# Attention and a routed expert layer on one core: the instruction order planned anew, the last pair's moves by engine copies, and another dependency for the first GpSimd rotation

## The chip, the core and the metric

The kernel runs on one core of a Trainium2 chip. A core has a matrix engine (PE), and VectorE (DVE), ScalarE (ACT) and GpSimd (POOL) for work on tiles; SyncE (SP) here issues DMA transfers. Each engine takes its own instructions strictly in order and waits at an instruction until the data that it needs are there. The metric is the device time of one execution in microseconds (us). Before the change its median was 584.03 us over 3 runs (583.14 to 585.76).

## The reference

For 8 batches, 8 heads, 576 positions and 64 values per head: q and k are turned by position, attention is computed per head, and the heads of a position are put side by side to rows of 512. Then, in each batch, the 128 rows with the highest gate score go through a two-layer network and are added, weighted, to themselves.

```python
def _attn_ref(q, k, v):
    ...
    q_rot, k_rot = (rotate(q), rotate(k))
    scores = (1.0 / np.sqrt(D)) * np.matmul(q_rot, k_rot.transpose(0, 1, 3, 2))
    scores = scores - np.max(scores, axis=-1, keepdims=True)
    attn = np.exp(scores)
    attn = attn / (np.sum(attn, axis=-1, keepdims=True) + 1e-09)
    return np.matmul(attn, v)
def _moe_ref(x, w_gate, w1, w2, capacity):
    scores = np.einsum('bsd,d->bs', x, w_gate)
    out = x.copy()
    for b in range(B):
        top_idx = np.argpartition(-scores[b], capacity)[:capacity]
        xe = x[b, top_idx]
        ye = np.maximum(xe @ w1, 0.0) @ w2
        g = 1.0 / (1.0 + np.exp(-scores[b, top_idx]))
        out[b, top_idx] = x[b, top_idx] + g[:, None] * ye
```

## The kernel before

The work is cut into 32 pairs of heads, four pairs to a batch.

**Rotation.** For each pair k and q come by DMA (L481) into one buffer each, `k_in` and `q_in`. POOL multiplies them by the tables (L504), adds the halves (L510, L514), ACT rounds the sum to a high part (L519), and POOL subtracts that to make a low part (L520, tiles `kl` and `ql`). For pair 0 DVE does this in smaller pieces.

**Scores.** A score step (L570) multiplies high and low parts, three products, for two of the nine row groups of a pair, or for the one that both heads share; a pair has five steps. DVE takes the row minimum of the negated scores (L591), ACT the exponential (L599), and DVE turns the result into `pt` in blocks of 32 (L622).

**Moves.** In each of a pair's two areas of `pt` two blocks must change their partitions. ACT or POOL copies one aside (L628), and four DMA moves per area on SP's queue do the change (L654). For the second area of the last pair the moves are copies of 32 partitions by ACT or POOL instead (L639), two for each half of each row group.

**Values and rows.** One value product for each area (L681), copied out (L356, L358), turned back to rows (L734), divided by the sums (L749, L753) and stored. The value tile `vt` also needs a copy to other partitions (L476), by ACT or POOL.

**Experts.** After each fourth pair come the gate scores (L821), a transpose for routing (L831), counting (L840, L853), a selection (L888) and the index products (L896). POOL casts the index (L911) and gathers the rows (L912) by an indirect DMA into `xe`; PE transposes them (L930), three-term expert products follow (L958, L977), DVE adds the result (L993), and POOL scatters the rows (L997). `xe` is a single buffer, so a gather cannot start until the scatter before it has read it. The experts' products of one batch are spread over the score steps of the next pairs. The weights get high and low parts during the first pairs (ACT L1022, POOL L1024).

**The order.** The code records every operation with a cost on each engine that may do it, a key (a due time, from `KEY`) and the operations that it comes after. `Order.run` then plays these costs forward, gives each free engine the ready operation with the lowest key, and so fixes both the order on each queue and which engine does a piece. The keys of each pair get random noise of 300 from a list of seeds, `SEEDS`. Where PE would be idle and has been busy for less than a share `warm` of a window, the plan puts in dummy matmuls (L367). `LANDED` is the time that the plan adds to the end of a transfer. The dependencies given to the plan decide the order alone: what an instruction waits for on the chip is set afterwards, from the tiles that it reads and writes.

The list that this change touches first is filled in `rotate` of pair 0, and read for pair 1:

```python
            if first:
                last_first.append(y)
...
        wait = list(last_first) if pi == 1 else []
```

Here `y` is a sum (L510, L514) and `d` the low part (L520).

Of the kernel before, what the change touches and what calls it, by code (L numbers as in the profile page):

```python
# [20 lines left out]
EPS = 1e-9  # L21


KEY = dict(warm=0.86, warm0=20000, warm1=1000000, dummy=430, dcols=256, ahead=15000, lag=16000, rem=400, value=17500, rows=5250, load=30500, rotate=173549, half=2500,
           gate=10237, route=21900, count=23781, select=5425, turn=24609, step=11400, count_=24062, select_=3000, turn_=98437, step_=10820, last_step=4750, kstep=2700, hold=3,
           vcopy=6000, lift=range(9), lifted=688, patience=900, over=450, near=-900, swap=9750, vsplit=9, vstep=2250, recip=7500, pool_lo=1, esplit=1, t_most=4, ring="SP", vring="SP", wring="SP", issue=250, svc0=800, svc1=200, svck=2101, svcq=2251, svcv=1501, first_moves=True, over_dma=750, patience_dma=1150)


SEEDS = (65, 53, 848, 188, 64, 106, 182, 56, 412, 765, 334, 840, 49, 811, 920, 630, 707, 350, 158, 580, 649, 829, 598,
         159, 606, 89, 919, 466, 149, 808, 916, 981, 466)  # L30
NOISE = 300.0


# [11 lines left out]
class Order:  # L45
# [4 lines left out]
    SEM = 45.0  # L50
    BLOCK, FETCH = 256, 3900.0
    WINDOW, FALL, RISE = 3413.0, 0.58, 0.88
    LANDED, FLYING = 500.0, 8


    TURN = {(a, b): t for t, froms, tos in (
# [222 lines left out]
def attention_moe_kernel(ctx: ExitStack, tc: tile.TileContext, q, k, v, gate, w1, w2, rope, outs, shape, cap):  # L279
# [32 lines left out]
    n_pairs = B * NP  # L312
# [146 lines left out]
    last_first = []  # L459
# [29 lines left out]
    def rotate(pi):  # L489
# [12 lines left out]
        def part(use, sum_use, sum_, tab, hu, lu, c0, c1, got, more=0):  # L502
            x, n = use.tile, c1 - c0
            m = op(time(2 * n), lambda: e.tensor_tensor(  # L504
                x[:, :, c0:c1], x[:, :, c0:c1], tab[:, :, c0:c1], op=ALU.mult), key + more, got)
            edge = name == "q" and c1 == S

            def add():
                m1 = MAIN if edge else c1
                e.tensor_tensor(sum_[:, c0:m1], x[:, 0, c0:m1], x[:, 1, c0:m1], op=ALU.add)  # L510
                for h in range(2) if edge else ():
                    hp = slice(64 * h, 64 * h + 64)
                    a, b = (x[hp, i, MAIN:S].rearrange("p (a j) -> p a j", j=32) for i in range(2))
                    e.tensor_tensor(striped(sum_)[hp, :, h], a, b, op=ALU.add)  # L514

            y = op(time(n) if not edge else {"DVE": dve(n, 1, 200.0)} if first else {"POOL": pool(MAIN, 540.0)}, add, key + more, [m] + sum_use.before)
            d1 = KW if edge else c1
            n = d1 - c0
            c = op({"ACT": act(n)}, lambda: nc.scalar.copy(hu.tile[:, c0:d1], sum_[:, c0:d1]), base + more, [y] + hu.before)  # L519
            d = op(time(n), lambda: e.tensor_tensor(  # L520
                lu.tile[:, c0:d1], sum_[:, c0:d1], hu.tile[:, c0:d1].bitcast(F32), op=ALU.subtract), base + more + 3000 * first, [c] + lu.before)
            use.by(m, y), sum_use.by(y, c, d), hu.by(c, d), lu.by(d)
            if first:
                last_first.append(y)
            return c0, d1, [c, d]

        whole = ((0, S),)
# [18 lines left out]
    def attend(pi):  # L546
# [64 lines left out]
        def turn(u, key):  # L611

            c = 1 if u == 8 else u // 4
# [15 lines left out]

            y = op({"ACT": act(L, 30), "POOL": pool_copy(L)}, aside_of, key, [o] + side_[c].before)  # L630
            area[c].by(o, y), side_[c].by(y)
            if not c or pi < n_pairs - 1:
                return [o, y]
            for g in (0, 2):
                e, o_ = slice(32 * g, 32 * g + 32), slice(32 * g + 32, 32 * g + 64)
# [8 lines left out]
        def move(c, key, turns):  # L644
# [13 lines left out]

            up = {g: (slice(32 * g, 32 * g + 32), slice(32 * g + 32, 32 * g + 64)) for g in (0, 2)}
            turns = sum(turns, [])  # L660
            if c and pi == n_pairs - 1:
                return
            gone = {g: part(g, two[e, 1], two[o_, 0], turns) for g, (e, o_) in up.items()}
            for g, (e, o_) in up.items():
# [109 lines left out]
        step = PAIR / len(UNITS)  # L774
# [377 lines left out]
```

## Time and profile before

| | |
|---|---|
| timed runs, median of 3 | 584.03 us |
| profiled execution | 578.55 us |
| its span, first to last instruction | 576.5 us |
| granted PE clock, mean of the span | 0.99 |
| matmul instructions of L367 (dummies) | 95, as 190 records |
| moves of the last pair by DMA | 4 of 8 |

The profile is one execution. A row of the time line gives the start, the duration, the engine, the line, the operation with what it writes and reads, and in brackets the idle time of the engine just before it with what ended it. A matmul in float32 appears as two records. Rows that follow each other on one line are merged with a count.

### The profile page before, as it was taken

Reading aid. Unit: us, or ns where it says so; the run is one execution under the profiler, and the core shown is the slowest. Engines: PE = TensorE matmul, PEld = TensorE weight load, DVE = VectorE, ACT = ScalarE, POOL = GpSimd, SP = SyncE. Lnnn points to the kernel's source line nnn. Section 1 sums busy time; section 2 is a strip of 40 time slices with the busy share of each in tenths; the row PEclk is TensorE's granted clock in tenths of the full one; section 3 lists DMA queues with packets and bytes.
Section 4 is the critical chain, followed back from the end, with each engine's and each line's share of the span. In section 5 each row is a group of like instructions: output and inputs, shape, how many; then the busy total and the mean of one; then the engine's idle time right before and its main releaser. Section 6 shows DMA issues by size and latency. Waiting matters only on the chain.

```text
span 576.5 us, 19632 instructions
## 1 busy us (share of the span) xinstructions
PE 534.2 (93%) x7558; PEld 443.7 (77%) x7558; DVE 494.2 (86%) x1249; ACT 478.2 (83%) x1307; POOL 452.1 (78%) x489
## 2 busy tenths in 40 slices
PE   2799999999999899989999999986999899999996
PEld 1587787788788688878788877765888787888885
DVE  7887899999999899988999979994999898989331
ACT  4788899999997999889998979785898998979521
POOL 2989999999998987969897998857899688825310
PEclk9989999999999999999999999997999999999999
DMA  7477887888676866676777687764776768555210
GB/s 238 136 215 223 238 240 214 244 221 240 197 225 189 227 175 194 198 234 192 198 224 197 185 213 177 191 195 131 219 198 193 227 178 214 156 131 157 63 38 18
DMA packets 56957, 108.67 MB, mean 189 GB/s; under 512 B 7072, under 2 KB 37664, under 8 KB 56864
## 3 DMA queue, kind: packets, MB, share of 16 engines
q1 hardware_dynamic: 54768, 102.58, 63.4%
q0 software_dynamic: 1280, 4.20, 2.4%
q8 instruction: 59, 0.97, 0.7%
q10 hardware_dynamic: 816, 0.66, 0.4%
q14 instruction: 34, 0.28, 0.2%
HBM read 54.14 MB, written 11.53 MB: 114 GB/s over the span
## 4 chain that ended last, share of the span: by engine, by line
PE 31%; ACT 19%; DMA 14%; POOL 14%; issue 11%; DVE 9%; SPq 1%; POOLq 0%; DVEq 0%; ACTq 0%
PE ps L681 9%; PE ps L570 9%; ACT pab L599 8%; PE ps L958 7%; DMA out_dram<-xe,idx 5%; DVE pab L591 3%; POOL q_in L504 3%; DVE pt L622 3%; DMA pt<-pt 3%; DMA k_in<-k_dram 3%; ACT pt L628 3%; DMA xe<-out_dram,idx 3%; PE ps L734 2%; POOL k_in L504 2%; ACT vt L476 2%
## 5 line engine op out<-in xcount | busy, mean ns | idle before, releaser
L599 ACT ACTIVATE pab<-pab,nm 128x576 f32<-128x576 f32 x256 | 197.1, 773 | 19.8 <-DVE pab L591 18.4
L622 DVE STREAM_TRANSPOSE pt<-pab 128x576 f32<-128x576 f32 x256 | 189.5, 761 | 17.4 <-ACT pab L599 15.9
L591 DVE TENSOR_SCALAR_CACHE_REDUCE pab<-ps 128x576 f32<-128x576 f32 x256 | 181.0, 745 | 22.8 <-PE ps L570 22.5
L681 PE MATMUL ps<-pt,vt 64*64 64x128 f32 (+1 forms) x4608 | 158.7, 286 | 2.5 <-ACT gp L751 1.8
L681 PEld LDWEIGHTS ps<-pt,vt 64*64 64x64 f32 x4608 | 140.8, 133 | 17.0 <-issue 6.5
L570 PE MATMUL ps<-kh,qh 64*128 64x288 f32 (+1 forms) x576 | 89.3, 352 | 13.7 <-ACT qh L519 10.2
L628 ACT COPY pt<-pt 128x288 f32<-128x288 f32 x220 | 87.9, 431 | 13.8 <-DVE pt L622 8.6
L504 POOL TENSOR_TENSOR k_in<-k_in,tabs 128x1152 f32<-128x1152 f32 x31 | 82.7, 2666 | 16.5 <-DMA k_in<-k_dram 15.9
L570 PEld LDWEIGHTS ps<-kh,qh 64*128 64x128 f32 (+1 forms) x576 | 51.2, 190 | 47.5 <-issue 12.8
L504 POOL TENSOR_TENSOR q_in<-q_in,tabs 128x1152 f32<-128x1152 f32 x31 | 82.8, 2669 | 3.4 <-DMA q_in<-q_dram 3.0
L570 PE MATMUL ps<-kh,ql 64*128 64x288 f32 (+1 forms) x576 | 71.3, 299 | 3.9 <-POOL ql L520 2.0
L570 PE MATMUL ps<-kl,qh 64*128 64x288 f32 (+1 forms) x576 | 70.7, 296 | 0.0
L570 PEld LDWEIGHTS ps<-kh,ql 64*128 64x128 f32 (+1 forms) x576 | 53.8, 190 | 4.7 <-POOL ql L520 2.5
L958 PE MATMUL ps<-w,xt 128*128 128x512 f32 x192 | 54.4, 413 | 0.0
L570 PEld LDWEIGHTS ps<-kl,qh 64*128 64x128 f32 (+1 forms) x576 | 53.9, 191 | 0.0
L734 PE MATMUL ps<-turner,ot 128*128 128x136 f32 x320 | 50.0, 287 | 3.6 <-ACT ot L356 3.0
L958 PE MATMUL ps<-w,ht 128*128 128x512 f32 x192 | 52.3, 409 | 0.0
L367 PE MATMUL ps<-tabs,turner 128*128 128x256 f32 x190 | 51.9, 398 | 0.0
L734 PEld LDWEIGHTS ps<-turner,ot 128*128 128x128 f32 x320 | 43.1, 189 | 10.5 <-ACT ot L356 4.8
L520 POOL TENSOR_TENSOR ql<-q_sum,qh 128x640 fp32r<-128x640 f32 x31 | 48.4, 1560 | 2.0 <-ACT qh L519 2.0
L599 ACT ACTIVATION_READ_ACCUMULATOR pab<-pab,nm 128x1 f32 x256 | 49.0, 191 | 0.0
L520 POOL TENSOR_TENSOR kl<-k_sum,kh 128x576 fp32r<-128x576 f32 x31 | 44.1, 1423 | 3.2 <-ACT kh L519 2.5
(110 smaller groups left out, 775.7 us busy)
## 6 DMA issues: line engine op xcount, KB each, us to landing
pt<-pt SPq DMA_DIRECT2D x124, 180.0 KB
pt<-pt SPq DMA_DIRECT2D x128, 144.0 KB
k_in<-k_dram SPq DMA_DIRECT2D x31, 576.0 KB
q_in<-q_dram SPq DMA_DIRECT2D x31, 576.0 KB
vt<-v_dram SPq DMA_DIRECT2D x32, 288.0 KB
out_dram<-x SPq DMA_DIRECT2D x16, 512.0 KB
xe<-w_dram SPq DMA_DIRECT2D x8, 256.0 KB
h<-w_dram SPq DMA_DIRECT2D x8, 256.0 KB
```

The costliest lines, as they stand in the source:

```text
L367: nc.tensor.matmul(bank_of(b)[:, 0:KEY["dcols"]], ident, tabs[:, 0, 0:KEY["dcols"]], start=True, stop=True)
L476: (nc.gpsimd.tensor_copy if e == "POOL" else nc.scalar.copy)(use.tile[mine, 1], use.tile[there, 0])
L504: m = op(time(2 * n), lambda: e.tensor_tensor(x[:, :, c0:c1], x[:, :, c0:c1], tab[:, :, c0:c1], op=ALU.mult), key + more, got)
L520: d = op(time(n), lambda: e.tensor_tensor(lu.tile[:, c0:d1], sum_[:, c0:d1], hu.tile[:, c0:d1].bitcast(F32), op=ALU.subtract), base + more ...
L570: nc.tensor.matmul(bank_of(bs[i])[:, n, 0:HALF], lt, rt, start=start, stop=stop)
L591: nc.vector.tensor_scalar(halves, bank_of(b)[:, :, 0:HALF], -1.0, None, op0=ALU.mult, op1=ALU.min, accum_out=nm.tile[:, u:u + 1])
L599: lambda: nc.scalar.activation(halves, halves if lift else bank_of(b)[:, :, 0:HALF], AF.Exp, bias=nm.tile[:, u:u + 1], scale=-1.0 if lift ...
L622: nc.vector.transpose(into, src.rearrange("p (m w j) -> p m w j", w=2, j=32))
L628: (nc.gpsimd.tensor_copy if e == "POOL" else nc.scalar.copy)(apart(c)[:, to * L:to * L + L], two)
L681: nc.tensor.matmul(bank_of(acc)[64 * h:64 * h + 64, g, c0:c0 + 32 * n], vt.tile[gp_, h ^ g, (m - 1) % 2 * NT + (m - 1) // 2 if m else 2 * ...
L734: nc.tensor.matmul(bank_of(b)[:, W * i:W * i + W], ot.tile[:, i * P:i * P + P], turner, start=True, stop=True)
L958: nc.tensor.matmul(bank_of(bank), lhs.tile[:, a, c * P:c * P + P], w[w_][:, c, fs], start=(c == 0 and i == 0), stop=(c == n - 1 and i == 2))
```

## The change

Three edits of the code. Pair 0's low parts `d` join the sums in the list that pair 1's rotation comes after. The first area of the last pair is moved by copies (L639) too, so its four moves at L654 are gone and sixteen copies are new. And the plan's numbers are others: `LANDED`, 20 entries of `KEY` (a few of them: `warm`, `load`, `rotate`, `turn_`, the service times of transfers) and all seeds.

```diff
-KEY = dict(warm=0.86, warm0=20000, ..., rows=5250, load=30500, rotate=173549, half=2500,
+KEY = dict(warm=0.82, warm0=20000, ..., rows=3750, load=27500, rotate=216936, half=6250,
...
-    LANDED, FLYING = 500.0, 8
+    LANDED, FLYING = 1250.0, 8
...
             if first:
-                last_first.append(y)
+                last_first.extend((y, d))
             return c0, d1, [c, d]
...
             area[c].by(o, y), side_[c].by(y)
-            if not c or pi < n_pairs - 1:
+            if pi < n_pairs - 1:
                 return [o, y]
             for g in (0, 2):
...
             turns = sum(turns, [])
-            if c and pi == n_pairs - 1:
+            if pi == n_pairs - 1:
                 return
             gone = {g: part(g, two[e, 1], two[o_, 0], turns) for g, (e, o_) in up.items()}
```

In the built programs the dummies go from 95 to 80, the copies of 32 partitions from 14 to 24 on POOL and from 6 to 12 on ACT, the moves from 252 to 248. All other work is the same in kind and number, but for small pieces that go to another engine.

On DVE, in pair 0, where `ql_85` is the second low part of q and L591 the row minima (- before, + now):

```order
 L514 TENSOR_TENSOR q_sum_78<-q_in_75 64x2x32 x2
-L591 TENSOR_SCALAR pab_89,nm_101<-ps 128x576 x2
+L591 TENSOR_SCALAR pab_89,nm_101<-ps 128x576
 L520 TENSOR_TENSOR ql_85<-q_sum_78,qh_83 128x512
-L622 STREAM_TRANSPOSE pt_92<-pab_89 128x9x2x32 x2
-L591 TENSOR_SCALAR pab_90,nm_101<-ps 128x576 x2
```

The low part now stands between the first two row minima in place of behind them.

On POOL, at the fourth scatter (L997) and the fifth gather (L912), with the semaphores that each instruction waits for; DMASW7 is the scatter's. Before:

```order
L997 DMA out_dram<-xe_110,idx_114 576x512 [waits DVE_49,Pool_49]
L476 COPY vt_87<-vt_87 64x576 [waits DMAHW0_49,PE_49]
L628 COPY pt_92<-pt_92 128x288 [waits DMAHW4_49,DMAHW5_49,DVE_49,Pool_49]
L628 COPY pt_92<-pt_92 128x288 [waits DVE_49]
L716 COPY sums_99<-sums_99 32x1 [waits Activation_49]
L716 COPY sums_99<-sums_99 32x1 [waits DMASW7_49,Pool_49]
L716 COPY sums_99<-sums_99 32x1 x2
L911 CAST idx_113<-gg_117 128x1 [waits Pool_49]
L912 DMA xe_110<-out_dram,idx_113 128x512 [waits DMAHW3_49,DMAHW2_49,Pool_49]
L504 TENSOR_TENSOR q_in_75<-q_in_75,tabs 128x1152 [waits DMAHW3_49]
```

And at the same place now:

```order
L997 DMA out_dram<-xe_110,idx_114 576x512 [waits DVE_49]
L476 COPY vt_87<-vt_87 64x576 [waits DMASW7_49,DMAHW7_49,PE_49,Pool_49]
L628 COPY pt_92<-pt_92 128x288 [waits DVE_49,Pool_49]
L504 TENSOR_TENSOR q_in_75<-q_in_75,tabs 128x1152 [waits DMAHW1_49]
L911 CAST idx_113<-gg_117 128x1 [waits DVE_49]
L912 DMA xe_110<-out_dram,idx_113 128x512 [waits DMAHW0_49,Pool_49]
```

The wait for the scatter moved from a small copy to the first copy behind the scatter, and a q multiply came ahead of the gather.

On PE, ahead of the transposes of the fifth gather (L930). The value products (L681) of two areas, score steps (three rows of L570 each), rows out (L734) and dummies (L367). Before:

```order
L681 MATMUL ps<-pt_92,vt_88 64x128 x36
L570 MATMUL ps<-kh_79,qh_83 128x288 x4
L570 MATMUL ps<-kl_81,qh_83 128x288 x4
L570 MATMUL ps<-kh_79,ql_85 128x288 x4
L367 MATMUL ps<-tabs,turner 128x256
L734 MATMUL ps<-turner,ot_94 128x136 x2
L367 MATMUL ps<-tabs,turner 128x256
L570 MATMUL ps<-kh_80,qh_84 128x288 x4
L570 MATMUL ps<-kl_82,qh_84 128x288 x4
L570 MATMUL ps<-kh_80,ql_86 128x288 x4
L681 MATMUL ps<-pt_93,vt_88 64x160 x36
L930 MATMUL ps<-turner,xe_110 128x128 x4
```

And now:

```order
L681 MATMUL ps<-pt_92,vt_88 64x128 x36
L367 MATMUL ps<-tabs,turner 128x256
L570 MATMUL ps<-kh_80,qh_84 128x288 x4
L570 MATMUL ps<-kl_82,qh_84 128x288 x4
L570 MATMUL ps<-kh_80,ql_86 128x288 x4
L734 MATMUL ps<-turner,ot_94 128x136 x2
L681 MATMUL ps<-pt_93,vt_88 64x160 x36
L570 MATMUL ps<-kh_80,qh_84 128x288 x4
L570 MATMUL ps<-kl_82,qh_84 128x288 x4
L570 MATMUL ps<-kh_80,ql_86 128x288 x4
L930 MATMUL ps<-turner,xe_110 128x128 x4
```

A dummy went, and the second area's product now stands ahead of a score step that is the next pair's second in place of its first.

## Rows read from the trace of the kernel before

**Rows 1.** The page's busy times: engine, us, share of the span, instructions.

```profile
PE 534.2 (93%) x7558; PEld 443.7 (77%) x7558; DVE 494.2 (86%) x1249; ACT 478.2 (83%) x1307; POOL 452.1 (78%) x489
```

**Rows 2.** Groups by form, dummies: records, busy us, mean ns, idle before.

```profile
L367 PE MATMUL ps<-tabs,turner 128*128 128x256 f32 x190 | 51.9, 398 | 0.0
```

**Rows 3.** Time line of PE and POOL at pair 2 and pair 8.

```profile
46.30 0.53 PE L570 MATMUL ps<-kh,ql 64*128 64x288 f32 x4 [0.43 <-POOL ql L520]
...
133.92 1.57 POOL L520 TENSOR_TENSOR ql<-q_sum,qh 128x640 fp32r<-128x640 f32 x1
...
141.30 0.53 PE L570 MATMUL ps<-kh,qh 64*128 64x288 f32 x4
```

**Rows 4.** Busy us by engine, between index products: first, fourth, fifth cycle, sum.

```profile
119.60:182.50 62.90, 62.15 (x936) 52.25 (x935) 60.00 (x153) 57.92 (x159) 59.91 (x62) 1.00 0.77 224
...
311.40:376.80 65.40, 62.89 (x931) 52.07 (x929) 59.34 (x151) 55.94 (x158) 56.52 (x61) 1.00 0.74 199
376.80:447.40 70.60, 63.38 (x932) 53.14 (x931) 60.00 (x153) 57.51 (x156) 56.12 (x64) 0.95 0.66 186
...
sum 392.60, PE 374.50 PEld 312.56 DVE 358.94 ACT 346.39 POOL 330.17; mean PE 62.42 PEld 52.09 DVE 59.82 ACT 57.73 POOL 55.03
```

**Rows 5.** Waits of PE: us in total, times, longest.

```profile
PE ps L930 <- DMA xe<-out_dram,idx: 13.1, 4, 7.2
```

**Rows 6.** Time line of PE and POOL, fourth scatter to fifth gather.

```profile
367.51 2.34 PE L958 MATMUL ps<-w,ht 128*128 128x512 f32 x9
...
377.45 1.06 POOL L997 DMA_INDIRECT out_dram<-xe,idx  x1 [0.28 <-POOL q_sum L514]
...
385.76 0.61 POOL L716 COPY sums<-sums 32x1 f32<-32x1 f32 x3 [5.39 <-DMA out_dram<-xe,idx]
...
387.28 1.06 POOL L912 DMA_INDIRECT xe<-out_dram,idx  x1 [0.66 <-POOL idx L911]
...
393.55 1.11 PE L930 MATMUL ps<-turner,xe 128*128 128x128 f32 x4 [7.22 <-DMA xe<-out_dram,idx]
```

**Rows 7.** Time line of POOL and DVE in pair 0; group of the smaller low part.

```profile
12.78 2.64 POOL L504 TENSOR_TENSOR k_in<-k_in,tabs 128x1152 f32<-128x1152 f32 x1 [10.35 <-DMA k_in<-k_dram]
...
13.61 2.35 DVE L520 TENSOR_TENSOR ql<-q_sum,qh 128x512 fp32r<-128x512 f32 x1
...
L520 DVE TENSOR_TENSOR kl<-k_sum,kh 128x288 fp32r<-128x288 f32 x2 | 0.9, 454 | 0.5 <-ACT kh L519 0.5
```

**Rows 8.** Groups of POOL by form.

```profile
L504 POOL TENSOR_TENSOR q_in<-q_in,tabs 128x1152 f32<-128x1152 f32 x31 | 82.8, 2669 | 3.4 <-DMA q_in<-q_dram 3.0
...
L510 POOL TENSOR_TENSOR k_sum<-k_in 128x576 f32<-128x576 f32 x31 | 44.1, 1423 | 0.9
...
L628 POOL COPY pt<-pt 128x288 f32<-128x288 f32 x68 | 28.1, 427 | 15.7 <-DVE pt L622 9.1 <-issue 5.4
...
L1024 POOL TENSOR_TENSOR w<-h,w 128x512 fp32r<-128x512 f32 x8 | 10.3, 1287 | 0.9 <-ACT w L1022 0.9
```

**Rows 9.** Chain of waits: value products of the two areas, a score step.

```profile
370.32 2.61 PE ps L681 x72
372.92 0.99 PE ps L570 x12
...
402.18 2.12 PE ps L681 x72
```

**Rows 10.** Line L997 (scatters), then line L912 (gathers), issue to landing.

```profile
DMA to landing us min/median/max: 2.7/5.5/8.2
...
DMA to landing us min/median/max: 3.4/4.3/6.2
```

**Rows 11.** Time line of POOL and PE in the last pair.

```profile
531.42 5.87 POOL L639 COPY pt<-pt 32x288 f32<-32x288 f32 x13
...
536.88 5.10 PE L681 MATMUL ps<-pt,vt 64*64 64x160 f32 x144
```

More of the change, by code (lines that the diff above doesn't have):

```diff
@@ L21 @@
 EPS = 1e-9
[L24 to L30, printed above, removed]
+KEY = dict(warm=0.82, warm0=20000, warm1=1000000, dummy=430, dcols=256, ahead=15000, lag=16000, rem=400, value=17500, rows=3750, load=27500, rotate=216936, half=6250,
+           gate=10237, route=21900, count=23781, select=6175, turn=24609, step=11400, count_=24062, select_=2250, turn_=110741, step_=10820, last_step=3250, kstep=2700, hold=3,
+           vcopy=6000, lift=range(9), lifted=688, patience=1400, over=450, near=-1500, swap=8531, vsplit=9, vstep=3000, recip=7500, pool_lo=1, esplit=1, t_most=4, ring="SP", vring="SP", wring="SP", issue=250, svc0=725, svc1=176, svck=1901, svcq=1901, svcv=1051, first_moves=True, over_dma=1050, patience_dma=150)
+SEEDS = (75, 786, 401, 197, 403, 214, 769, 676, 423, 679, 34, 190, 614, 927, 237, 430, 597, 975, 828, 799, 53, 919,
+         936, 170, 592, 220, 580, 277, 76, 507, 377, 813, 460)
 NOISE = 300.0
```

## Prediction

> **What bounds the kernel now.** I read first the page's busy times, then stretches cut at the index products (L896) of one batch after the next, then what TensorE (PE) waits for, and last the time line around the longest of those waits.
>
> PE is busy for 93% of the span, VectorE (DVE) for 86% [rows 1]. PE's share holds 95 dummy matmuls, 51.9 us, 0.55 us each [rows 2]: the plan puts them where PE would stand idle, so they are idle time in disguise. Without them PE has 482 us of work, less than DVE's 494. No engine is full by itself; what costs is the places where one waits.
>
> The stretches tell three parts apart. Up to the index products of the first batch (119.6 us) there is attention alone, bounded by GpSimd (POOL), which rotates q and k and makes the low parts of the expert weights: pair 2's scores wait for its last low part [rows 3]. By pair 8 that is over: its low part ends at 135.5 us and is first used at 141.3, a margin of 5.8.
>
> From 119.6 to 512.2 us lie six cycles of four pairs and one batch of experts, 392.6 us. The shortest, 62.9, leaves PE 0.75 us of idle time; the fifth takes 70.6 and leaves 7.2 [rows 4]. PE waits 13.1 us in all at L930, the transposes of the gathered rows, four times, 7.2 at the worst [rows 5]. How that comes about is seen in the fifth cycle [rows 6]. The last expert product of the old batch ended at 369.85, DVE adds it to the rows, POOL scatters them at 377.45, and three of POOL's four small copies behind it stand still for 5.4 us until the scatter has landed; only then come the index cast and the next gather, 387.28, because both transfers use the one buffer xe. PE, which takes its queue in order, got to the transposes at 386.33 and stood until 393.55. The chain from product to transposes took 23.7 us, PE's own work in between 16.5. After this wait the granted clock of the cycle is 0.95, and PE's busy time is 63.4 against a mean of 62.2 in the other five, 1.1 us more.
>
> The last part, 64 us, is the last pairs and the experts of two batches; PE is nearly full there.
>
> **The change part by part.** Three edits of the text: a dependency of the first POOL rotation, four DMA moves made into copies, and new numbers for the plan. The last moves nearly every instruction.
>
> *The first rotation's wait.* Dependencies in this list order the plan; the chip waits only for data. In the built program the first POOL multiply waits for the same three semaphores in both kernels, the landing of k and DVE's sum, and it now starts at 12.78 us, when k lands [rows 7]. What does change is that DVE makes the last low part of pair 0 one reduction earlier, so at 12.82 in place of 13.50. It took 2.35 us there, where a part of a similar kind, without POOL beside it, took 0.45 for 288 columns in the same trace, 0.8 for 512 in proportion: POOL's multiply ran from 12.78 to 15.42, and the low part ended at 15.96. If the multiply still starts first, the low part ends at 15.96 again and now the second reduction stands behind it, up to 2.4 us later; if the low part comes first, PE gets it some 2.3 us earlier. I take 0 for both: pair 2's scores still wait for POOL at 46.3 us [rows 3], so that work covers it. Without that cover it is −2.3 to +2.4.
>
> The Trainium skill ("SBUF — State Buffer", Who interferes with whom) says that a VectorE instruction with two SBUF inputs and a GpSimd instruction that reads SBUF exclude each other for the whole instruction, and the one that starts later waits. By it the low part, ready 0.04 us after the multiply, loses again and the edit gains nothing; the 15.96 agrees with it.
>
> *First part.* Nothing is removed from POOL's queue but its order is new. Ahead of pair 4's low parts stand three weight parts (1.29 each) and one k multiply, k sum and q multiply fewer, 10.6 us [rows 8]; ahead of pair 7's two weight parts fewer and one copy more, 2.1; ahead of pair 8's one q multiply and one k sum more and a copy less, +3.7. So the lead of 10 us is given back by pair 7. The 16 dummies fewer up to the first L930 (62 to 46) are worth nothing by themselves, since POOL sets the pace. The index products come behind 34 score steps in place of 33, one step of 0.99 more [rows 9]. For pair 6, in which they fall, POOL is 1.6 ahead (12 weight parts in place of 15 and four casts of 0.2 fewer, one q multiply and one copy more): −1.6 + 1.0 = −0.6. Bounds: −2.1, and +3.7 if pair 8's margin of 5.8 is gone. The first gather stands 7.7 us further back on POOL (two multiplies, one q sum, one copy), but PE has 17.4 us of work between index products and L930, 11.3 before, so it is covered.
>
> *The six cycles.* Dummies: 23 become 28, +2.7 us. Score steps: 121 become 120, −1.0. The waits at L930: by counting PE's instructions between the last expert product and L930, with the durations of [rows 9], dummies at 0.5 and rows out at 0.44 and 0.67, PE's own work is 15.8, 15.8, 20.2, 16.7, 16.3 us for the second to sixth gather before (the trace gives 16.5 at the fifth) and 21.5, 18.3, 18.7, 18.3, 19.2 in the new order. Against it stands the chain. The scatter leaves 4.6 to 7.6 us after the product (5.3 in the mean of five). At the fifth and sixth gather POOL now has, behind the scatter, a value copy that waits for its landing, then 0.4 of copy, a multiply of 2.67, the cast and 0.7 of start: landing 5.5 in the median [rows 10], then 4.6, then the gather's 4.3, with the 5.3 19.6 us. That is 1.3 and 0.4 more than PE's work. At the second gather DVE's addition is 2.9 later and the chain 22.1: 0.6. At the third and fourth PE's work is longer than the chain. Sum 2.3 in place of 13.1. With the longest landings of [rows 10], 8.2 and 6.2, each chain is 4.6 longer and the waits are 17.7. I take 5: nearer the median, since one boundary of five had both long. The lost clock goes with the long wait, −0.9 of its 1.1. So +2.7 − 1.0 − 8.1 − 0.9 = −7.3; bounds −13 (no wait left) and +6 (17.7 of waits, no clock regained).
>
> *The last pair.* Four DMA moves become 16 copies of 32 partitions (10 more on POOL, 6 on ACT). The value product of the second area waited for POOL's 13 copies, which ended at 537.29; the first area's stood behind it, and both were through at 541.98 [rows 11]. Ten copies more on POOL are 4.5 us at the row's 0.45; between none and all of it falls into idle time of POOL, so it ends between 537.3 and 541.8; I take the middle, 539.5. But the first area's product, 2.1 us, now comes ahead of the second's, in time in which PE ran dummies; with 2.6 for the second, both are through at 542.1, where they were. Behind them 12 expert products in place of 9 stand ahead of the routing transposes, 0.8 us at 0.27 each. What is issued no longer are four of SP's moves, which nothing waits for last here. I take +0.5; bounds −1.5 (the copies hidden, the product's 2.1 saved) and +2 (the copies stack up).
>
> Sum: −0.6 − 7.3 + 0.5 = −7.4. The profiled execution has 578.55 us, a span of 576.5 and 2.05 around it; the median of the timed runs is 584.03, 5.5 above. The sum is taken off the median: 576.6 us.
>
> **The rivals.**
>
> *The wait only changes its place: no gain.* DVE works 59.3 to 60.0 us in each cycle; to save 7 it has to reach 93 to 94% over all of them. For it: the fourth cycle had no wait at L930 and still took 65.4. Against: the first took 62.9. Then it is the fifth cycle alone at best, spent on five dummies and later reductions: 583.5. The Trainium skill ("Perfetto Trace Analysis", Identifying the Most-Contended Engine) holds the share of busy matmuls for a bad measure of TensorE's headroom and looks at weight loads, 77% here; then VectorE is the fullest engine, with work that the change leaves as it is. By that rule this rival is the outcome.
>
> *The scatter holds POOL: slower.* At the fifth and sixth gather the first copy behind the scatter waits for its landing, where three or four small ones went ahead before; a 2.67 us multiply then stands ahead of the gather. If the landings are as in the fifth cycle (8.2 and 6.2), the waits are 17.7 and the cycles cost +6.3: 590. It decides from waits of 12 us on, which is some 2.9 us above the median landings for the two together.
>
> *The change doesn't do what it says.* The first multiply doesn't wait; this is what I expect, at no cost. If it does wait, pair 1's low parts come up to 0.7 later: 577.3 at most. It has no chance of its own.
>
> *All of it lands.* No wait left, first part −2.1: 569.
>
> **How the numbers follow.** Forecast 576.6, own range 571 to 581: 0.56. All lands, 569: 0.08. No gain, 583.5: 0.18. Slower, 590: 0.18. What a measurement of this kernel can tell from no change is about 0.5%, 2.9 us: faster is below 581.1, slower above 586.9. Faster: nearly all of the first two, 0.63; same 0.19; slower 0.18. Range 567 to 588: below it a part of the best case, above it most of the slower one.
>
> **What would show it.** Right: waits at L930 of 3 to 7 us in place of 13.1; the six cycles from index products to index products sum to 383 to 388 us; none above 67; first index products at 118 to 121; the last pair's copies end at 538 to 541; the first POOL multiply starts with the landing, and the low part beside it again takes over 2 us. Wrong: a wait above 5 us at the fifth or sixth gather behind a value copy; POOL low parts late again at pair 8; cycles at 65 without any wait at L930, which would make DVE's pace the bound.

## The result and the profile after

The changed kernel takes 587.34 us (median of 21 runs, 580.56 to 591.62), the kernel before 582.12 (21 runs, 576.53 to 585.76): a ratio of 1.0093, 95% interval 1.0068 to 1.0119. It is slower; the forecast was 576.6 and faster. The ratios leave out executions more than 1.5% above the fastest of their kernel, the changed kernel's profiled one among them and, further down, one of 1350.93 us.

The profiled execution of the changed kernel took 589.97 us, 2.6 above its median, that of before 578.55, 3.6 below its own; two profiles set side by side show 11 us where the medians show 5. A third one helps: the changed order with one VectorE instruction moved, which changes no time (first experiment), was profiled at 583.63, 0.1 from its median, when the median of before stood at 578.73, close to the profile of before. I read the stages from that.

| us | before | changed | changed, one moved |
|---|---|---|---|
| to the first index products | 119.6 | 121.3 | 119.4 |
| six cycles | 392.6 | 398.8 | 396.1 |
| from the seventh index products on | 64.3 | 67.8 | 66.1 |

By the last column nothing is lost in the first part, some 3.5 us in the cycles, some 1.8 in the tail. Cycles and tail, of before and of the changed order with one moved, columns as in [rows 4]:

```profile
119.60:512.16 392.56, 374.46 (x5580) 312.52 (x5578) 358.90 (x902) 346.39 (x955) 330.17 (x355) 0.99 0.71 199
512.16:576.50 64.34, 59.37 (x716) 49.44 (x714) 32.81 (x86) 31.87 (x93) 17.76 (x44) 0.99 0.28 76
```

```profile
119.42:515.47 396.05, 376.74 (x5579) 314.45 (x5577) 359.67 (x911) 343.30 (x942) 334.20 (x358) 0.98 0.71 197
515.47:581.60 66.13, 59.01 (x716) 49.32 (x714) 32.54 (x88) 33.91 (x97) 20.99 (x50) 1.00 0.22 63
```

The page of the changed kernel, the busy times (before: [rows 1]):

```profile
PE 535.7 (91%) x7528; PEld 443.6 (75%) x7528; DVE 495.2 (84%) x1253; ACT 478.0 (81%) x1298; POOL 456.3 (78%) x496
```

POOL has 4.2 us more work, the others within 1.5 us of before; no share has grown, those of PE, VectorE and ScalarE fell by 2 points each. Stretches of the changed kernel: first part, fifth cycle, tail:

```profile
0.00:121.26 121.26, 98.86 (x1238) 80.53 (x1239) 101.77 (x257) 99.43 (x260) 101.09 (x90) 0.94 0.76 211
...
382.87:452.22 69.35, 63.55 (x929) 53.09 (x928) 60.22 (x152) 58.08 (x160) 55.58 (x63) 0.95 0.70 193
...
520.09:587.90 67.81, 60.23 (x716) 50.50 (x714) 32.68 (x88) 33.96 (x97) 21.16 (x50) 0.96 0.22 64
```

The fifth cycle is 1.3 us shorter than it was (69.35 against 70.60), and its granted clock is 0.95 again. Waits of PE in the changed kernel, answering to [rows 5], and in the changed order with one moved:

```profile
PE ps L930 <- DMA xe<-out_dram,idx: 10.1, 4, 5.0
```

```profile
PE ps L930 <- DMA xe<-out_dram,idx: 11.5, 4, 5.5
```

Time line of the changed kernel around the longest of them, answering to [rows 6]:

```profile
372.97 3.06 PE L958 MATMUL ps<-w,ht 128*128 128x512 f32 x12
...
379.23 0.71 DVE L993 SCALAR_TENSOR_TENSOR xe<-ps,gg,xe 128x512 f32<-128x512 f32 x1
...
383.18 1.06 POOL L997 DMA_INDIRECT out_dram<-xe,idx  x1 [0.15 <-issue]
390.83 0.65 POOL L476 COPY vt<-vt 64x576 f32<-64x576 f32 x1 [6.58 <-PE ps L570]
...
391.94 2.66 POOL L504 TENSOR_TENSOR q_in<-q_in,tabs 128x1152 f32<-128x1152 f32 x1
...
395.00 1.08 POOL L912 DMA_INDIRECT xe<-out_dram,idx  x1 [0.27 <-POOL idx L911]
...
400.12 1.11 PE L930 MATMUL ps<-turner,xe 128*128 128x128 f32 x4 [5.01 <-DMA xe<-out_dram,idx]
```

From the product's end (376.03) to the transposes are 24.1 us; it was 23.7 before. The row of the value copy (L476) names PE, but that had long been done: the copy also waits for the scatter's landing (DMASW7 in the built program, shown above under the change), which the trace has at 390.61, 0.2 us ahead of the copy.

### The profile page after: what moved, and what is told of

It reads as the page before. It is cut to its first block, busy times and chain, and to the rows that moved or that the text cites. A ratio compares the mean times of both kernels' runs of the same rounds, so it can differ in the third digit from the quotient of the medians.

```text
span 587.9 us, 19570 instructions
## 1 busy us (share of the span) xinstructions
PE 535.7 (91%) x7528; PEld 443.6 (75%) x7528; DVE 495.2 (84%) x1253; ACT 478.0 (81%) x1298; POOL 456.3 (78%) x496
## 5 line engine op out<-in xcount | busy, mean ns | idle before, releaser
L599 ACT ACTIVATE pab<-pab,nm 128x576 f32<-128x576 f32 x256 | 197.5, 774 | 11.8 <-DVE pab L591 9.9
L591 DVE TENSOR_SCALAR_CACHE_REDUCE pab<-ps 128x576 f32<-128x576 f32 x256 | 180.7, 741 | 12.4 <-PE ps L570 11.5
L681 PE MATMUL ps<-pt,vt 64*64 64x128 f32 (+1 forms) x4608 | 162.6, 291 | 2.5 <-DMA pt<-pt 1.2
L681 PEld LDWEIGHTS ps<-pt,vt 64*64 64x64 f32 x4608 | 144.2, 136 | 17.4 <-issue 7.8
L570 PE MATMUL ps<-kh,qh 64*128 64x288 f32 (+1 forms) x576 | 91.1, 356 | 20.5 <-ACT qh L519 10.2
L570 PEld LDWEIGHTS ps<-kh,qh 64*128 64x128 f32 (+1 forms) x576 | 51.7, 192 | 55.1 <-issue 14.8
L570 PE MATMUL ps<-kh,ql 64*128 64x288 f32 (+1 forms) x576 | 71.9, 300 | 3.4 <-DVE ql L520 2.0
L570 PE MATMUL ps<-kl,qh 64*128 64x288 f32 (+1 forms) x576 | 71.8, 298 | 0.0
L570 PEld LDWEIGHTS ps<-kh,ql 64*128 64x128 f32 (+1 forms) x576 | 54.5, 192 | 4.0 <-DVE ql L520 2.3
L734 PE MATMUL ps<-turner,ot 128*128 128x136 f32 x320 | 50.9, 292 | 4.2 <-ACT ot L356 4.0
L570 PEld LDWEIGHTS ps<-kl,qh 64*128 64x128 f32 (+1 forms) x576 | 54.5, 192 | 0.0
L734 PEld LDWEIGHTS ps<-turner,ot 128*128 128x128 f32 x320 | 43.6, 194 | 10.0 <-ACT ot L356 6.5
L367 PE MATMUL ps<-tabs,turner 128*128 128x256 f32 x160 | 44.5, 401 | 1.1 <-ACT gp L751 0.8
```

What stands on the lines that cost most here:

```text
L367: nc.tensor.matmul(bank_of(b)[:, 0:KEY["dcols"]], ident, tabs[:, 0, 0:KEY["dcols"]], start=True, stop=True)
L570: nc.tensor.matmul(bank_of(bs[i])[:, n, 0:HALF], lt, rt, start=start, stop=stop)
L591: nc.vector.tensor_scalar(halves, bank_of(b)[:, :, 0:HALF], -1.0, None, op0=ALU.mult, op1=ALU.min, accum_out=nm.tile[:, u:u + 1])
L599: lambda: nc.scalar.activation(halves, halves if lift else bank_of(b)[:, :, 0:HALF], AF.Exp, bias=nm.tile[:, u:u + 1], scale=-1.0 if lift ...
L681: nc.tensor.matmul(bank_of(acc)[64 * h:64 * h + 64, g, c0:c0 + 32 * n], vt.tile[gp_, h ^ g, (m - 1) % 2 * NT + (m - 1) // 2 if m else 2 * ...
L734: nc.tensor.matmul(bank_of(b)[:, W * i:W * i + W], ot.tile[:, i * P:i * P + P], turner, start=True, stop=True)
```

## The experiments

The ratios are to the kernel before, timed alongside on the same chip, 95% interval in brackets; medians of different experiments are not compared. A diff shows the lines that matter; three dots mark what is cut. Where a kernel has added lines, its line numbers are a little higher (L571 for L570, L682 for L681, L735 for L734).

**The first low part's place.** The changed order, with the low part behind the second row minimum again:

```diff
...
+    plan.insert(to_, plan.pop(at_))
...
```

> The changed kernel with one instruction moved: on VectorE, pair 0's last low part stands behind the second row minimum again, as before the change; every other instruction is where the change put it. If the first edit is worth nothing (the prediction's value), the time is the changed kernel's 587.3 us within 1. If the first pair's path to its scores sets the start, it moves by 2 us or more, in either direction. It is also a second profile of the changed order: if the loss over before is spread over the six cycles, these add up to 395 us or more against 392.6, and the part ahead of the first index products and the tail are each 1 to 3 us longer than before.

Measured: 583.77 us, 1.0084 (1.0048 to 1.0121): no difference from the changed kernel's 1.0093. Time line of VectorE and POOL, of the changed kernel and then of this one:

```profile
13.23 3.13 DVE L520 TENSOR_TENSOR ql<-q_sum,qh 128x512 fp32r<-128x512 f32 x1
...
13.18 2.64 POOL L504 TENSOR_TENSOR k_in<-k_in,tabs 128x1152 f32<-128x1152 f32 x1 [10.75 <-DMA k_in<-k_dram]
```

```profile
14.46 2.34 DVE L520 TENSOR_TENSOR ql<-q_sum,qh 128x512 fp32r<-128x512 f32 x1
...
13.62 2.63 POOL L504 TENSOR_TENSOR k_in<-k_in,tabs 128x1152 f32<-128x1152 f32 x1 [11.20 <-DMA k_in<-k_dram]
```

Both low parts end about 0.5 us after the multiply does, wherever they stand (16.36 against 15.82 us, 16.80 against 16.25). By the rule of the Trainium skill ("SBUF — State Buffer", Who interferes with whom) the one that starts later waits, and these traces agree. The edit of the list itself does less still: planned with the changed numbers, the list with `d` and the list without it give the same program, instruction for instruction on every engine. So what differs in time comes from the numbers and from the last pair's copies.

**The last pair's copies.** The edit undone in the changed kernel (the diff), and done alone in the kernel before; the order is planned anew only around the last pair:

```diff
-            if pi < n_pairs - 1:
+            if not c or pi < n_pairs - 1:
...
-            if pi == n_pairs - 1:
+            if c and pi == n_pairs - 1:
```

> The changed kernel with the second edit undone: the last pair's first area is moved by four DMA moves again; the order up to the last pairs is the changed one, only the order around the last pair's work is planned anew. The tail from the seventh index products to the end was 64.3 us before and 67.8 in the changed kernel's profile. If the sixteen copies are what made it longer, this gives back 2 to 3.5 us: 584 to 585. If the tail is longer because the work ahead of it was late and the copies are hidden, as the prediction had it at +0.5, the time stays within 1 of 587.3.

> The kernel before with the second edit alone: the last pair's first area is moved by sixteen copies too; the order up to the last pairs is that of before. In profiles near their medians the tail from the seventh index products on took 64.3 us before, 66.1 in the changed order, and 63.4 in the changed order with the four DMA moves back. If the copies cost this: tail 66 to 67, 1.002 to 1.005 of before. If they are hidden, as the prediction had it to within 0.5 us: tail 64 to 65, 0.999 to 1.002.

Measured: 582.70 us, 1.0084 (1.0050 to 1.0117) undone; 581.04, 1.0026 (0.9990 to 1.0062) alone. Tails, from the seventh index products to the end, undone in the changed kernel and alone in before:

```profile
512.23:575.60 63.37, 58.27 (x716) 49.19 (x714) 32.31 (x86) 32.36 (x95) 16.66 (x42) 1.00 0.27 76
```

```profile
512.08:579.20 67.12, 59.80 (x718) 49.70 (x716) 33.13 (x87) 33.73 (x96) 21.20 (x50) 0.99 0.24 67
```

Both ways the tail differs by 2.7 to 2.8 us (66.1 to 63.4; 64.3 to 67.1), and a third pair further down has 2.4. The medians do not separate it from nothing (1.0084 against 1.0084 to 1.0093; 1.0026 with 1 in its interval), and the profile with the edit undone lies 5.4 us below its kernel's median: the tails show the cost, the timed runs do not confirm it. As the list changes nothing, the kernel with the copies undone is before with the new numbers alone, and it takes 1.0084: the numbers, that is the new order, are slower by themselves.

**Waits of ScalarE for moves.** A second buffer for the blocks put aside, used by every other pair:

```diff
...
-        apart = lambda c: pts[c][:, side_[c].tile:side_[c].tile + (4 + c) * L]
+        apart = lambda c: pts[c][:, side_[c].tile + pi % 2 * (4 + c) * L:side_[c].tile + (1 + pi % 2) * (4 + c) * L]
...
```

> The changed kernel in the same order on every engine, with a second buffer for the blocks put aside, used by every other pair, so that a copy aside need not wait until the moves of the pair before have landed (to make room half of the experts' low weight parts share a place, so those low parts are wrong; the work is the same). In the changed kernel's profile ScalarE stands 17.5 us in front of such copies for a move to land, 4.2 before the change. Theory one, moves that land later than planned hold ScalarE and through it VectorE and TensorE: the 17.5 fall below 2 and the time falls by 3 to 5 us, to 582.5 to 584.5. Theory two, ScalarE has slack (81% busy) and its waits are only where it rests: the time stays within 1 of 587.3.

Measured: 583.96 us, 1.0103 (1.0056 to 1.0150). In the changed order ScalarE stood 20.0 us there; with two buffers no such row is left. The changed order's row, then the longest wait of ScalarE with two buffers:

```profile
ACT pt L628 <- DMA pt<-pt: 20.0, 11, 5.4
```

```profile
ACT pab L599 <- DVE pab L591: 14.5, 28, 2.8
```

The wait goes and the time stays: theory two. ScalarE's wait was slack, idle time that nothing behind it was waiting for.

**Dummies.** Left out ahead of 60 us in the kernel before; then all of them, without the bound on `t`, in both orders:

```diff
-    for _, _, o, e in order.run():
+    for t, _, o, e in order.run():
+        if o.fn.__name__ == "dummy" and t < 60000:
+            continue
```

> The kernel before without the dummy matmuls that its plan puts ahead of 60 us; everything else in the same order. In the changed kernel, with 16 fewer up to the first gather, the granted clock fell to 0.50 to 0.78 between 36 and 54 us, and there was no such fall in the kernel before. If that fall costs time at the start, this kernel is 1.5 to 4 us slower than before, 583.5 to 586, with the same fall of the clock. If GpSimd's low parts set the pace there, as the prediction had it, the clock falls and the first index products still come at 119 to 120.5 us, and the time stays within 1 of before.

> The kernel before without any of the 95 dummy matmuls, all else in the same order. Leaving out the 27 ahead of 60 us made it 0.8% faster, though the clock there fell to half for some stretches. Theory one, a dummy stands in TensorE's queue ahead of real work that the plan thought late: without the 23 in the six cycles these are up to 12 us shorter unless the clock falls; 1 to 3% under before. Theory two, they keep the clock up: without them it falls in the cycles as it did after the 7 us wait (0.95 of a cycle, 1.1 us each), and the time is level with before or up to 1.5% slower.

> The changed kernel without any of its 80 dummy matmuls, all else in the same order. The changed order has 28 of them in the six cycles where before had 23, counted as 2.7 us in the prediction. Theory one, they are real work on the path: the cycles shorten by up to 14 us, and the gap to the kernel before without dummies is about 0.4 points smaller than the 0.9% with them. Theory two, they keep the clock up and cost nothing: level or slower, and the gap stays 0.9%.

Measured: 574.02 us, 0.9919 (0.9885 to 0.9952) without the early ones; 577.35, 0.9949 (0.9915 to 0.9983) without any in before; 586.13, 1.0104 (1.0058 to 1.0150) without any in the changed order. Without the early ones the granted clock fell as foretold, to 0.64 to 0.85 in four of the five stretches of 6 us from 30 to 60 (before had 0.79 in the first of them and 1.00 in the others), and the first index products came at 120.1: no cost there, but a gain that neither theory had. One of these stretches, and the deepest of the changed kernel:

```profile
42.00:48.00 6.00, 2.94 (x28) 2.33 (x20) 3.57 (x11) 4.86 (x11) 6.00 (x5) 0.71 0.72 208
```

```profile
36.00:42.00 6.00, 5.50 (x84) 5.17 (x84) 3.44 (x9) 4.02 (x9) 3.56 (x5) 0.50 0.91 289
```

Without any, the gap between the orders is 1.55 points (1.0104 less 0.9949); theory one had it shrink and theory two had it stay at 0.9, and it grew. So the changed order's five more dummies in the cycles are not what makes it slower. The two without any show the difference best: their profiles are 8.6 us apart, as much as the ratios say. Their six cycles, before and changed, and PE's longest waits in each:

```profile
119.50:510.90 391.40, 368.85 (x5534) 308.04 (x5533) 358.44 (x905) 346.34 (x958) 330.69 (x355) 0.98 0.71 200
```

```profile
PE ps L930 <- DMA xe<-out_dram,idx: 11.8, 4, 4.9
PE ps L570 <- ACT ot L356: 2.1, 4, 0.8
PE ps L734 <- ACT ot L356: 1.9, 3, 0.9
PE ps L570 <- DVE pab L591: 1.4, 4, 0.5
...
PE ps L681 <- DMA pt<-pt: 0.2, 1, 0.2
```

```profile
120.60:517.60 397.00, 368.82 (x5523) 308.55 (x5522) 360.44 (x911) 343.44 (x940) 332.54 (x357) 0.98 0.70 194
```

```profile
PE ps L930 <- DMA xe<-out_dram,idx: 11.6, 4, 4.5
PE ps L570 <- DVE pab L591: 3.4, 5, 1.1
PE ps L681 <- DMA pt<-pt: 3.0, 3, 1.6
PE ps L734 <- DVE ot L358: 2.2, 2, 1.3
```

PE's busy time is the same to 0.03 us, the waits at L930 to 0.2. All of the 5.6 us between the cycles is idle time of PE, and it lies in short waits: for landed moves +2.8 us, for row minima ahead of score steps +2.0, for data of the experts +2.2; those of rows out (L734) fell by 1.1.

**The waits at the gathered rows.** A second buffer for them, in both orders:

```diff
...
+        if b % 2 and not last:
+            xe.tile = xe2
...
```

> The changed kernel in the same order on every engine, with a second buffer for the gathered rows, used by every other batch, so that a gather need not wait until the scatter before it has landed (half of the experts' second-layer low weight parts share a place to make room, so those are wrong; the work is the same). TensorE's waits at L930 were 10.1 us in the changed kernel's profile and 11.5 in that of the run with the low part moved back; the prediction had counted on 5. Theory one, these waits are full time of the kernel: they fall below 2 us, the six cycles from 396 to 386 to 389, the time 1.2 to 1.7% below the changed kernel's, so level with before or up to 0.8% under it. Theory two, other engines are as full: what TensorE doesn't wait there it waits in front of score steps and rows out, and the time stays within 0.4% of the changed kernel's.

> The same second buffer in the kernel before (same order, same low parts wrong). Its waits at L930 were 13.1 us. Theory one: they fall below 2, the time 1.5 to 2.2% under before. Theory two: within 0.5% of before. If before gains more than the changed kernel does, the changed order had indeed already taken some of these waits away and lost elsewhere; if both gain alike, the change took none away.

Measured: 583.82 us, 1.0080 (1.0044 to 1.0116), and 575.79, 0.9928 (0.9896 to 0.9961). The premise failed: the waits stayed, in the changed order 8.2 us (fifth and sixth gather), in before 11.1, for POOL still stood behind the scatter at an instruction that has nothing to do with the rows. So the shared buffer was not what held the gather, as the prediction had it; why the built program puts the wait there is not shown. That before gained 0.7%, more than the 2.0 us of waits that went, is not explained. The changed order's value copy, as in the time line above:

```profile
387.26 0.66 POOL L477 COPY vt<-vt 64x576 f32<-64x576 f32 x1 [6.10 <-PE ps L735]
```

So the gather of batches 1 to 6 was put directly behind the scatter, into the buffer h, idle then; ScalarE copies the rows to xe later:

```diff
-                out=xe.tile[0:n], out_offset=None, in_=outs[b],
+                out=rows_of(b, xe)[0:n], out_offset=None, in_=outs[b],
...
+            nc.scalar.copy(xt.tile[:, 0], bank_of(bx))
+            if 0 < b < B - 1:
+                nc.scalar.copy(xe.tile, rows_of(b, xe))
...
+        plan[from_:at_ + 1] = mid + [plan[at_]] + late + plan[ix + 1:at_]
...
```

> The changed kernel with the gathers of batches 1 to 6 going into the experts' buffer h, which is free then, right behind the scatter on GpSimd's queue (cast and gather first, the value copies, aside copies and multiplies that stood between behind them); ScalarE copies the rows into xe later (512 columns, six times). All else in the same order. The second buffer alone had left 8.2 us of waits at the transposes of the gathered rows, since GpSimd still stood at a value copy until the scatter had landed. Theory one, these waits are time of the kernel: they fall below 3 us and the time by 6 to 9 us, to 0.994 to 0.999 of before. Theory two, in the changed order other waits (row minima, moves, rows out) are as late and take their place: within 0.4% of the changed kernel's 1.009.

> The same in the kernel before: gathers into h right behind the scatter. Its waits at the transposes were 13.1 us, 11.1 with the second buffer, which gained 0.7%. Theory one: below 3 us, the time 1.5 to 2.2% under before. Theory two, other waits take over: 0.990 or above, no better than the second buffer's 0.993 by more than noise.

Measured: 584.56 us (median of five executions), 1.0109 (1.0044 to 1.0174), and 571.17, 0.9835 (0.9783 to 0.9887). In both the waits for the rows are gone. Before gains 1.65%, the changed order nothing that shows (its interval leaves room for some 0.5%). POOL still stands at the same copy; what changed is that the gather has gone out ahead of it, 2.5 us after the scatter's start in place of 11.8:

```profile
382.35 1.05 POOL L913 DMA_INDIRECT h<-out_dram,idx  x1 [0.66 <-DMA q_in<-q_dram]
388.59 0.66 POOL L477 COPY vt<-vt 64x576 f32<-64x576 f32 x1 [5.19 <-DMA h<-out_dram,idx]
```

Six cycles and tail, of before so altered and of the changed order, each with PE's longest waits in the cycles:

```profile
121.41:508.28 386.87, 375.76 (x5580) 311.21 (x5579) 358.42 (x902) 347.87 (x960) 330.28 (x355) 1.00 0.72 201
508.28:572.80 64.52, 59.14 (x716) 49.57 (x714) 32.89 (x86) 32.34 (x94) 17.69 (x44) 1.00 0.27 76
```

```profile
PE ps L682 <- DVE pab L592: 2.1, 2, 1.7
PE ps L571 <- DVE pab L592: 2.0, 5, 0.8
```

```profile
120.11:513.70 393.59, 378.16 (x5579) 312.16 (x5577) 361.36 (x911) 345.49 (x947) 333.92 (x357) 1.00 0.72 198
513.70:580.70 67.00, 59.23 (x716) 49.44 (x714) 32.88 (x88) 34.39 (x98) 21.47 (x50) 1.00 0.22 64
```

```profile
PE ps L571 <- DVE pab L592: 3.6, 4, 2.3
PE ps L735 <- ACT ot L356: 2.8, 4, 1.0
PE ps L983 <- ACT h L979: 2.5, 4, 1.2
PE ps L682 <- DMA pt<-pt: 1.8, 4, 1.1
```

The granted clock is 1.00 in all four stretches. The cycles differ by 6.7 us: 2.4 are PE's busy time (five more dummies, one score step less), 4.3 its idle time (15.4 against 11.1, span less busy). The tail differs by 2.5. The profile of before so altered lies 3.3 us above its median, the other 2.0 below its own: they are 8 us apart where the ratios say 2.7 points, so not all of the difference is located. Nor is before's gain all waiting: its cycles are 5.7 us shorter for 13.1 us of waits gone, and its six timed executions have a mean clock of 0.989 to 0.997 where before has 0.976 to 0.991 beside them; what the clock gives of the 1.65% was not separated.

**What the order alone costs, without waits for the rows.** The same changed order with the four moves back as well:

> The changed kernel with two of its suspected costs out at once: gathers into h right behind the scatter, and the last pair's four DMA moves back. What is left against the kernel before with the same gathers (0.9835) is the new order alone. If small waits and five more dummies in the six cycles are the loss (in the profiles 393.6 against 386.9 us without waits at the gather), it is at 1.003 to 1.008, tail 63.5 to 65 us. If the copies were the larger part, it comes to 0.995 or below.

Measured: 581.25 us, 1.0044 (1.0007 to 1.0081). Cycles and tail:

```profile
120.12:514.09 393.97, 377.90 (x5579) 313.05 (x5577) 361.25 (x911) 346.18 (x949) 334.32 (x358) 1.00 0.71 199
514.09:578.70 64.61, 59.04 (x716) 49.37 (x714) 32.46 (x86) 32.91 (x96) 17.10 (x42) 1.00 0.26 75
```

The four moves are worth 2.4 us by the tails, and 0.65 points by the ratios, whose intervals overlap. What is left against before with the same gathers is the new order alone: 1.0044 to 0.9835 by ratios from two chips, 5.9 us by the spans of the two profiles.

**Which numbers.** The kernel before with one set of the changed numbers at a time:

```diff
-    LANDED, FLYING = 500.0, 8
+    LANDED, FLYING = 1250.0, 8
...
```

> The kernel before with one number changed, LANDED 1250 in place of 500, and so planned anew from the first transfers on. If planning with later landings is good by itself, this is faster than before by 0.3% or more and the waits on landed moves shorter. If the loss comes with it, 1.005 to 1.01. Rival: any new plan from the same costs is a new draw, and since the other numbers were kept with 500, this one is slower by anything between 0.3 and 2%, with waits that grow at places that have nothing to do with landings (row minima, rows out).

> The kernel before with the changed kernel's seeds alone; priorities, landing time and code as before. If the numbers belong together and before's are a selected set, this new draw is 0.3 to 2% slower, with the six cycles 3 us or more longer and the tail as before (64 to 65.5 us). If seeds are only noise around the same order, within 0.3%.

> The kernel before with the changed kernel's priorities alone (the twenty entries, the shorter service times of transfers among them); seeds, landing time and code as before. If the priorities carry the loss, 1.005 to 1.015 and the seeds' run is near 1.000. If every new draw loses, both are slower by 0.3 to 2%. If the changed priorities are better and only the seeds fit them badly, this one is at 1.000 or below.

Measured: landing time alone 591.90 us, 1.0194 (1.0133 to 1.0255); seeds alone 589.93, 1.0154 (1.0076 to 1.0231); priorities alone 605.23, 1.0435 (1.0371 to 1.0498). Landing time and priorities alone are each worse than all three sets together; the interval of the seeds overlaps theirs. The 4.35% of the priorities is more than any theory had. Six cycles of the run with the priorities alone, and PE's longest waits in them:

```profile
128.55:538.85 410.30, 383.77 (x5576) 317.51 (x5574) 365.88 (x929) 342.44 (x922) 325.23 (x336) 0.98 0.67 187
```

```profile
PE ps L570 <- DVE pab L591: 6.2, 5, 2.9
PE ps L734 <- ACT ot L356: 5.6, 5, 1.9
PE ps L930 <- DMA xe<-out_dram,idx: 4.0, 3, 1.6
```

The slowest order of all waits 4.0 us for the gathered rows, before 13.1: these waits do not tell a good order from a bad one.

**Both gains together.** The kernel before with the gathers into h and without the early dummies:

> The kernel before with the gathers into h, and without the 27 dummy matmuls ahead of 60 us. If the two gains have different places they add up: 0.974 to 0.979. If what the run without early dummies gained (0.8%) was at the gathers, where its waits were 6.8 us against 13.1, they don't add up: 0.982 to 0.986.

Measured: 574.84 us, 0.9930 (0.9898 to 0.9962): it doesn't add up, lies above the ranges of both theories, and is no better than the early dummies' removal alone. Against the gathers into h alone (0.9835, six executions on another chip) the removal now loses a point, where it gained 0.8% by itself; why stays open. The two profiles with the gathers into h have spans of 572.8 and 573.1 us, so the gain of the gathers is better taken as 0.7 to 1.65%. The lowest ratio is that of before with the gathers into h.

## Why the prediction was wrong

- **The waits at L930, 13.1 to 5, −8.1 us: the step that failed.** They came to 10.1 and, in the profile near its median, 11.5. In the changed kernel they were 1.2, 1.3, 5.0 and 2.6 at the second, third, fifth and sixth gather, where the sum had 0.6, 0, 1.3 and 0.4. The chain of the fifth was taken link by link at the mean or median, 19.6 us; it took 24.1: the scatter left 7.2 us after the product (I had 5.3), POOL went on 7.65 after the scatter's start (5.5), the rows came 5.1 after the gather's (4.3). PE's own work before it was 19.1 (18.3). The reason that I gave for the chain, the one buffer xe, was not what held it: with two buffers POOL stood 6.1 us at the same copy.
- **What is late next: no term at all.** I let a microsecond less of waiting at L930 be a microsecond of the kernel. In the kernel before that is in part so (13.1 us of waits gone gave 1.65%, some 9 us, in the timed runs and 5.7 us in the profiled cycles); in the changed order all of these waits could go and no gain was seen. The other waits of PE had no term in the sum: its idle time is +4.3 us without the gather's waits, +5.6 without dummies. I counted instructions between two points on PE and did not look at how close the row minima, the moves and the experts' steps behind them now lay.
- **The size of the miss in the cycles.** In the profile near its median they came to +3.5 us for a forecast of −7.3. Of these 10.8 us, 6.5 are the waits at L930, 2.8 other idle time of PE, 1.5 its busy time.
- **The clock, −0.9: wrong.** The fifth cycle, with its wait of 5.0 us, still stood at 0.95.
- **Dummies and score steps, +2.7 − 1.0: right in size** as busy time, +2.4 where nothing else disturbs; as time of the kernel not borne out, since the gap between the orders was no smaller without any dummies.
- **The last pair, +0.5: mis-sized.** The tail grew by 1.8 us in all; the copies by themselves lengthen it by 2.4 to 2.8 us, beyond my +2. I had them half hidden; in the changed kernel's time line the last ends at 548.59, 28.5 us after the seventh index products, against 25.1 before [rows 11]. It waits for ScalarE's share of them, and the value product starts only behind it:

```profile
548.18 0.41 POOL L639 COPY pt<-pt 32x288 f32<-32x288 f32 x1 [0.80 <-ACT pt L639]
548.94 2.68 PE L681 MATMUL ps<-pt,vt 64*64 64x160 f32 x72
```

- **The first part, −0.6: right in substance**, −0.2 in the profile near its median, 1.7 late in the other. Dropping 27 dummies there did not move it either, which agrees with POOL setting that pace. **The first rotation: right**, 0, and the low part beside POOL's multiply took over 2 us again.
- **The base.** I took the sum off 584.03, the median of three; that of 21 is 582.12. From that the same sum gives 574.7, further off still.
- **The rivals.** "The scatter holds POOL" gave 590 and lies nearest in time, and its place (the fifth and sixth gather, behind a value copy) was real; but its price was not paid there: 10 to 11.5 us of waits, not 17.7, so that its number came near is luck. "The wait only changes its place" had the right mechanism for a part of what was missing, in small waits all over the cycles. Its reason, VectorE full, is not borne out: with the gathers into h before's six cycles fell from 392.6 to 386.9 us on the same VectorE work (358.4), so VectorE did not set the 392.6. The sign that I had named for it did appear (65.1 and 65.2 us in the changed kernel's first and fourth cycle, without a wait at L930), and VectorE was busy for 93% of the 386.9, so a limit not far below is not excluded. The Trainium skill's rule beside it ("Perfetto Trace Analysis", Identifying the Most-Contended Engine) pointed to VectorE; these cycles do not bear it out here.

Shown is that the new order by itself is slower, and that with the dummies out its loss in the cycles lies in many short waits of PE; which of its moved instructions makes them is not. That a new plan from these costs loses is shown for four sets of numbers, no more; that before's set had been picked among many is only a likely reason.

## What to carry to other kernels

Where a planner with noise in its keys fixes the order, new numbers are a new draw for every wait in the kernel: give the wait that you see in the profile no credit until an edit that keeps the order shows what it is worth, and price "what is late next" from the short waits, not only from the longest. Price a chain of transfers with its spread and not at its median: the fifth gather's took 24.1 us, where medians gave 19.6 and the longest landings 24.2. Issuing one gather ahead of the instruction that stands waiting, with the rest of the order kept, gained 0.7 to 1.65%, where the new plan was hoped to gain 1.3%.

## What the runs showed that I had not expected

- Behind an indirect DMA the built program lets a later POOL instruction wait until the transfer has landed, though that instruction uses none of its data (6.1 us at a value copy, with a buffer of its own for the rows). A second buffer did not take PE's waits away, putting the gather first did.
- 20.0 us of ScalarE's waits taken away were worth nothing that shows (1.0103 against 1.0084 to 1.0093).
- All 95 dummies could go from the kernel before with the granted clock at 0.98 in the cycles (0.93 ahead of them), and it was 0.5% faster.
